# Windowed attention and SwiGLU on one core: the RMS weight row first, half-block scores for the first two query blocks, and a new plan

## The chip, the cores and the metric

The kernel runs on one core of a Trainium2 chip. A core has five engines with a queue each: TensorE (matmuls, PE in the profile; its weight loads are shown as PEld), VectorE (DVE), ScalarE (ACT), GpSimd (POOL) and SyncE (SP), which here only issues DMAs. Sixteen DMA engines move data between HBM and the core's SBUF. Matmuls write to PSUM, which has eight banks of 512 f32 values per partition. The metric is the device time in microseconds (us); lower is better.

## The reference

Inputs are q, k and v of shape (4, 8, 768, 64) in f32: four batches, eight heads, 768 positions, 64 values per head. Attention is causal with a window of 128 positions and four sink positions that every query sees:

```python
scores = scale * np.matmul(q, k.transpose(0, 1, 3, 2))
keep = is_sink | in_window            # pos < 4, or 0 <= query - key < 128
a = softmax(np.where(keep, scores, -1e9))
attn = np.matmul(a, v)
x = attn.transpose(0, 2, 1, 3).reshape(3072, 512)
xn = x / sqrt(mean(x * x) + 1e-6) * rms_g
out = (silu(xn @ w_gate) * (xn @ w_val)) @ w_out   # d_ff = 1536
```

The result is 3072 x 512 in f32. What attention gives is not stored; it stays on the core as the x of the second part.

## The kernel before

**Tiling.** The 3072 tokens are 24 blocks of 128, numbered g = 0 to 23, six to a batch (t = g mod 6). A block of keys is seen by its own block of queries (mask: upper triangle) and by the next one (mask: lower triangle). So for each key block, scores are computed transposed, keys on the partitions, for two query blocks at once: n = 0 is the own block, n = 1 the next. One block has eight heads; `u` is a half of them (four), `hi` the upper or lower 64 partitions of the transposed q and k. Four token blocks form a group G of the feed-forward part (six groups). Its hidden size of 1536 is 12 chunks `ft` of 128.

**Stages of a block.** q and k are loaded, transposed (on TensorE for blocks 0 to 7, `pe_t` with `copy_t`; by DMA from SP after that), scored (`scores`), exponentiated on ScalarE (`exps`), masked, multiplied with V (`av`, with the sink positions as an extra matmul from t = 2 on), divided by the sum of the weights (`normal`), squared for the mean (`square`), scaled by the inverse RMS and the weight row (`rms`, which gives `xr`), and transposed to `xnt` (`pe_x` or `dma_x`). The feed-forward part is then gate matmuls `g` (weights `wg`), value matmuls `v` (`wv`, `mms` at L863), tanh on ScalarE (`th`, L870), two VectorE products (`p`, L876, and `hT`, L886), and the output projection `o` (L896). In the profile the V of attention and the value matmul's PSUM are both called v; the line tells them apart.

**Masks.** There are three ways to mask. For g below `PE_MASKS` a matmul (`mask_bias`, L450) puts -32768 into the PSUM banks before the scores are added. For blocks up to `POOL_MASK_FROM`, and for the first of each batch, VectorE multiplies the exps by 0/1 masks (`mask_dve`, L533, one instruction per half of the heads, both n). From `POOL_MASK_FROM` on, GpSimd selects (`mask_pool`, L538 for n = 0, L543 for n = 1, two instructions per half of the heads).

**The weight row.** `rms_g` is 512 values in one row (`grow`). A matmul of a column of ones with the row spreads it over 128 partitions (`unit_gb`, L411), and `scale_gb` scales it into `gb`, which `rms` reads (L613).

**Loads.** k and q of block 0 are loaded in f32 by SP (L327) and cast on an engine (L331). All other q, k, v (L335, L339) and weight loads (`wg` and `wv` L381, `wo` L387) cast to bf16 on the way and are issued by GpSimd in the order of the string `LOADS`: `q-1` is q of block 1, `qkv-2` the three of block 2, `w-0-2` chunks 0 and 1 of `wg`, then of `wv`. `DEPTH` 8 makes the n-th of these loads wait for the landing of the (n-8)-th.

**What sets the order.** Nothing is issued as it is written. Each operation is entered in `Plan` with its engine or engines, an assumed duration, what it needs and gives, a priority, and the PSUM banks that it takes and drops. `Plan.run` is a list scheduler: at each step it takes, over all engines, the operation whose assumed start is earliest, then the one of lowest priority number. The order found is then the order of each engine's instructions, and it picks the PSUM bank of each tile. On the chip each engine takes its own instructions in that order and waits on semaphores; the assumed durations play no part there. `gate_of` holds scores of block 8 and later back until a feed-forward chunk (`GATE_LEAD` chunks ahead) has been planned.

`SPLIT` names blocks 0 and 1: their scores are two operations, one per n, in the same four PSUM banks, whose columns are laid out by half of the heads and pair of n (two heads x 256). So an exp of one n reads half a bank (128 x 256), eight of them per block.

`WARM` is 30: matmuls on zeros that fill idle time of TensorE at the start.

Of the kernel before, what the change touches and what calls it, by code (L numbers as in the profile page):

```python
# [26 lines left out]
class Plan:  # L27
# [2 lines left out]

    LATE = 300
    RESERVE = 8
    HOP = {"PE": 40, "ACT": 35, "DVE": 35, "POOL": 90, "SP": 60}
    START = {"PE": 800, "ACT": 800, "DVE": 1030, "POOL": 1290, "SP": 800}

# [5 lines left out]
    def op(self, ways, needs=(), gives=(), prio=0.0, takes=(), drops=(), ring=None, work=0.0,  # L43
           mode=0):
        self.ops.append(dict(
            ways=ways, needs=set(needs), gives=tuple(gives), prio=prio, takes=tuple(takes),
            drops=tuple(drops), ring=ring, work=work, mode=mode, at=len(self.ops), ready=0,
        ))

    def land(self, ring, first, work):  # L50
# [19 lines left out]
    def run(self):  # L70
        free, users = dict(self.START), {}
        self.loads = sum(o["ring"] == "POOL" for o in self.ops)
        wait = {o["at"]: set(o["needs"]) for o in self.ops}
        cand = {e: [] for e in free}
        left = len(self.ops)
        for o in self.ops:
            for t in o["needs"]:
                users.setdefault(t, []).append(o)
            if not o["needs"]:
                for e in o["ways"]:  # L80
                    cand[e].append(o)
        busy, warm, mode, order = [], False, 0, []
        while left:
            first = None

            many = min(
                (o for o in cand["PE"] if len(o["takes"]) > self.RESERVE), default=None,
                key=lambda o: o["prio"],
            )
            for e, found in cand.items():  # L90
                for o in found:
                    k = len(o["takes"])
                    if k > len(self.banks):
                        continue
                    ready = o["ready"] + self.HOP[e] if o["ready"] else 0
                    if k:
                        ready = max(ready, sorted(self.banks.values())[k - 1] + 40)
                    start = max(free[e], ready)
                    if (k and many and o["prio"] > many["prio"] and start > many["ready"]
                            and len(self.banks) - k < len(many["takes"])):  # L100
                        continue
                    key = (start, o["prio"], ready, o["at"])
                    if first is None or key < first[0]:
                        first = key, e, o
            if first is None:
                raise RuntimeError("stuck: %s" % [
                    (o["gives"], list(wait[o["at"]])) for o in self.ops if o["at"] in wait
                ][:20])
            (start, *_), e, o = first
            for x in o["ways"]:  # L110
                cand[x].remove(o)
            wait.pop(o["at"])
            left -= 1
            ns, lat, fn = o["ways"][e]
            if e == "PE":
                busy = [(a, d) for a, d in busy if a > start - 3413]
                warm = start - free[e] < 4000 and (warm or sum(d for a, d in busy) > 3000)
                ns = ns if warm else 2 * ns
                if o["mode"] != mode:
                    ns, mode = ns + 110, o["mode"]  # L120
                busy.append((start, ns if mode != 2 else 0))
                lat = ns + 180
            for s in o["takes"]:
                i = min(self.banks, key=lambda i: (self.banks[i], i))
                del self.banks[i]
                self.held[s] = i
            free[e] = start + ns
            end = start + lat
            if o["ring"] is not None:
                end = self.land(o["ring"], end, o["work"]) + self.LATE  # L130
            for s in o["drops"]:
                self.banks[self.held[s]] = end + 12
            for t in o["gives"]:
                for x in users.pop(t, ()):
                    x["ready"] = max(x["ready"], end + 12)
                    w = wait[x["at"]]
                    w.discard(t)
                    if not w:
                        for way in x["ways"]:
                            cand[way].append(x)  # L140
            order.append((start, end, e, fn, o))
        return order
# [3 lines left out]
def kernel(  # L146
# [31 lines left out]
    SW = P // HP  # L178
    inv_sqrt_d = 1.0 / math.sqrt(D)
    F32_LOADS = ("ks0","qs0")  # L180
    GROW = "SP"
    CAST_DVE = 600
    MASKS_PRIO = -5
    POOL_AT = (1,2)
    DEPTH = 8
    LOADS = "q-1 k-1 v-0 w-0-2 v-1 qkv-2 qkv-3 w-2-4 w-4-6 w-6-8 w-8-9 w-9-10 w-10-12 qkv-4 wo-0-6 qkv-5 wo-6-12 qkv-6 qkv-8 qkv-7"
    LOADS += "".join(f" qkv-{g}" for g in range(9, NB))
    PE_MASKS = 2
    POOL_MASK_FROM = 16
    X_DMA_FROM = 8  # L190
    QK_DMA_FROM = 8
    LD = 16
# [1 line left out]
    LOAD_LEAD = 10  # L194
    LEAD_FROM = 10
    WARM = 30
    GATE_LEAD = 14
    T_LEAD = 4
    SPLIT = (0,1)
    CHUNKS = (4,2,2)  # L200
    GB_PRIO = 2000
    FUSE_FROM = 2
    GROW_PRIO = -80
    MERGE = (2,)

    const = ctx.enter_context(tc.tile_pool(name="const", bufs=1))
# [49 lines left out]
    def either(ways, *args, **kw):  # L256
        op({e: (ns, ns + LAT[e], fn) for e, (ns, fn) in ways.items()}, *args, **kw)
# [68 lines left out]
        T["st", name, g] = opool.tile([P, H, D], FP32, name="stage", tag="osb")  # L326
        eng.dma_start(out=T["st", name, g], in_=block_of(src, g))  # L327

    def cast(name, g, copy):
        T[name, g] = ld.tile([P, H, D], BF16, name=name)  # L330
        copy(out=T[name, g], in_=T.pop(("st", name, g)))  # L331

    def load_bf16(name, src, g):
        T[name, g] = ld.tile([P, H, D], BF16, name=name)
# [10 lines left out]
    for i, name in enumerate(F32_LOADS):  # L345
        n, g, e = name[0], int(name[2:]), {"s": "SP", "a": "ACT"}[name[1]]
        src, eng = q if n == "q" else k, {"SP": nc.sync, "ACT": nc.scalar}[e]
        op({e: (430, 1000, lambda n=n, src=src, g=g, eng=eng: load_f32(n, src, g, eng))},
           (), [(n + "st", g)], -90 + i, ring="HW", work=970)
        either({"DVE": (CAST_DVE, lambda n=n, g=g: cast(n, g, nc.vector.tensor_copy)),  # L350
                "ACT": (640, lambda n=n, g=g: cast(n, g, nc.scalar.copy))},
               [(n + "st", g), "table"], [(n, g)], -99)
    op({GROW: (430, 1000, lambda: {"SP": nc.sync, "ACT": nc.scalar}[GROW].dma_start(
        out=grow, in_=moe_rms_g.rearrange("(o d) -> o d", o=1)))}, (), ["grow"], GROW_PRIO,
        ring="HW", work=50)
    act(1290, None, (), ["table"], -80)

    issue = []
# [81 lines left out]
    def dma_t(n, g):  # L440
        b, t = divmod(g, NT)
        nc.sync.dma_start_transpose(
            out=qk_tile(b)[:, "qk".index(n), :, t * P:(t + 1) * P],
            in_=T.pop((n, g)).rearrange("p h d -> p (h d)"),
        )

    def mask_bias(g):
# [100 lines left out]
    def av(g, u):  # L548
        b, t = divmod(g, NT)
        pv = bank(("av", g, u))  # L550
        if t >= 2:
            nc.tensor.matmul(  # L552
                out=pv[:, 0:HW], lhsT=T["esk", g], rhs=T["vsk", b][:, 4 * u:4 * u + 4, :],
                start=True, stop=False, skip_group_check=True,
            )
        for j in range(2):
            for hi in range(2):
                h = 4 * u + 2 * j + hi
                x = 2 * hi + j
                dest = pv[:, (h - 4 * u) * VW:(h - 4 * u + 1) * VW]  # L560
                if t >= 1:
                    nc.tensor.matmul(  # L562
                        out=dest, lhsT=T["e", g - 1, u][:, x, 1, :],
                        rhs=V16[b][:, t - 1, h, :],
                        start=(t == 1), stop=False, skip_group_check=True,
                    )
                own = (T["e", g, u][:, x, 0, :] if t + 1 < NT
                       else T["el", g][:, hi * HP + 2 * u + j, :])
                nc.tensor.matmul(  # L569
                    out=dest, lhsT=own, rhs=V16[b][:, t, h, :],  # L570
                    start=(t == 0), stop=True, skip_group_check=True,
                )
        T.pop(("e", g - 1, u), None)
# [130 lines left out]
    def block_scores(g):  # L704
# [2 lines left out]
        nq = 2 if t + 1 < NT else 1  # L707
        pa = -1000.0 + 10 * g
        early = -20.0 + g if g < 2 * GB else 0.1 * g
        slots = [("s", g, u, hi) for u in range(2) for hi in range(2)]  # L710
        parts = [(0, 1), (1, 2)] if g in SPLIT else [(0, nq)]
        if g < PE_MASKS:
            pe(864, lambda g=g: mask_bias(g), [("bias", 0), ("bias", 1), "ident", "idnos"]
               + ([("qp", g), ("kp", g)] if g else []), [("mb", g)], pa, takes=slots)
# [47 lines left out]
    for g in range(NB):  # L762
# [8 lines left out]
            old += [("ss", b - 2, i) for i in ((2, 4) if b - 2 < 2 else (2,))]  # L771
        for n in "qk":
            if g < QK_DMA_FROM:
                pe(225, lambda n=n, g=g: pe_t(n, g), [(n, g), "ident"] + old, [(n + "p", g)],
                   pa, takes=[(n, g)])
                ways = {"DVE": (345, lambda n=n, g=g: copy_t(n, g, nc.vector.tensor_copy)),
                        "ACT": (470, lambda n=n, g=g: copy_t(n, g, nc.scalar.copy))}
# [247 lines left out]
```

## Time and profile before

| | |
|---|---|
| median of 11 runs | 245.17 us (244.77 to 245.89) |
| the profiled execution's own time | 245.15 us |
| its span (first to last instruction) | 243.4 us |
| TensorE busy | 235.1 us (97% of the span), 2116 matmuls |
| VectorE busy | 180.9 us (74%) |
| ScalarE busy | 131.2 us (54%) |
| GpSimd busy | 89.6 us (37%) |
| chain that ended last | TensorE 92%, VectorE 4%, ScalarE 1% |
| gate, value and output matmuls | 69.5, 71.1 and 65.4 us busy |
| VectorE masks (L533) | 26, 0.68 us each |
| GpSimd selects (L538) | 10, 0.64 us each |
| casting loads (L335, L339) | 70, issue 0.88 us each, 11.7 to 12.7 us from issue to landing |

A line of the profile gives the start (in a timeline) and the duration, the engine, the source line, the operation, `out<-in` by the program's names, shapes, and in brackets how long the engine was idle before it and what ended that. In the row of slices each digit is the busy share of a 6.1 us slice, in tenths. [...] A matmul's duration overlaps the next one's, so the spacing of starts tells more than the duration.

### The profile page before, as it was taken

What the parts mean: (1) busy time and instruction counts of PE and PEld (TensorE: products, weight loads), DVE (VectorE), ACT (ScalarE), POOL (GpSimd) and SP (SyncE); (2) the same over time, 40 slices, a digit from 0 to 9 for tenths busy, and PEclk for the clock granted to TensorE, in tenths of its full rate; (3) what the DMA queues carried; (4) which work ended last, traced back from release to release, by engine and by line L of the source; (5) the groups of instructions that cost most, each with busy time, mean ns of one, the idle gap of its engine ahead of it and who ended that gap; (6) DMA issues with size and microseconds to landing.
All of it is one profiled execution on the core that took longest, in us unless ns stands there. A gap on an engine that the chain in (4) does not pass through costs nothing.

```text
span 243.4 us, 5513 instructions
## 1 busy us (share of the span) xinstructions
PE 235.1 (97%) x2116; PEld 148.4 (61%) x2116; DVE 180.9 (74%) x481; ACT 131.2 (54%) x268; POOL 89.6 (37%) x116
## 2 busy tenths in 40 slices
PE   4988999999999999999999999999999999999994
PEld 2557997885788875587796544544554444444443
DVE  4269979996999999998898889896379760377700
ACT  4677565869684827575734574573553311333111
POOL 8986875596445556245511130321320000000000
PEclk9999999999999999999999999999999999999999
DMA  9999999999999999999999561110231002200022
GB/s 130 150 168 196 186 187 187 159 138 177 147 196 151 158 133 155 161 227 143 133 152 117 111 172 24 22 22 30 81 108 24 1 0 86 86 3 0 0 86 86
DMA packets 113579, 27.35 MB, mean 112 GB/s; under 512 B 103697, under 2 KB 110609, under 8 KB 113554
## 3 DMA queue, kind: packets, MB, share of 16 engines
q0 software_dynamic: 81760, 13.90, 78.6%
q1 hardware_dynamic: 31650, 12.99, 29.3%
q8 instruction: 16, 0.26, 0.4%
q10 hardware_dynamic: 144, 0.13, 0.2%
q14 instruction: 9, 0.07, 0.1%
HBM read 28.31 MB, written 6.29 MB: 142 GB/s over the span
## 4 chain that ended last, share of the span: by engine, by line
PE 92%; DVE 4%; ACT 1%; issue 1%; POOL 1%; POOLq 0%; DVEq 0%
PE v L863 25%; PE o L896 25%; PE g L863 25%; PE s L468 4%; PE av L569 2%; PE av L562 2%; PE s L450 1%; PE av L552 1%; PE o_last L914 1%; ACT e L516 1%; PE k L428 1%; PE gb L411 1%; PE q L428 1%; PE x L628 1%; DVE xr L613 1%
## 5 line engine op out<-in xcount | busy, mean ns | idle before, releaser
L863 PE MATMUL v<-xnt,wv 128*128 128x128 bf16 (+2 forms) x528 | 71.1, 282 | 0.0
L870 ACT ACTIVATE th<-g 128x512 bf16<-128x512 f32 x72 | 43.2, 599 | 49.2 <-PE g L863 46.6
L863 PE MATMUL g<-xnt,wg 128*128 128x128 bf16 (+2 forms) x528 | 69.5, 282 | 0.0
L896 PE MATMUL o<-wo,hT 128*128 128x512 bf16 x276 | 65.4, 379 | 0.0
L876 DVE SCALAR_TENSOR_TENSOR p<-th,g 128x512 bf16<-128x512 bf16 x72 | 48.0, 682 | 21.2 <-ACT th L870 20.9
L863 PEld LDWEIGHTS <-wg 128*128 128x128 bf16 x528 | 43.1, 98 | 19.1 <-issue 0.4
L863 PEld LDWEIGHTS <-wv 128*128 128x128 bf16 x528 | 43.0, 98 | 19.2 <-issue 0.5
L886 DVE TENSOR_TENSOR hT<-p,v 128x512 bf16<-128x512 bf16 x72 | 47.2, 680 | 1.5 <-PE v L863 0.7
L516 ACT ACTIVATE e<-s 128x512 bf16<-128x512 f32 (+1 forms) x88 | 43.8, 569 | 7.5 <-PE s L468 6.2
L896 PEld LDWEIGHTS <-hT 128*128 128x128 bf16 x276 | 25.3, 98 | 26.6 <-issue 1.5
L904 ACT ACTIVATE osb<-o 128x512 f32<-128x512 f32 x23 | 13.8, 601 | 23.6 <-PE o L896 23.6
L335 POOL DMA_DIRECT2D q<-in_q_dram x23 | 20.5, 891 | 14.5 <-DMA k<-in_k_dram 6.3
L339 POOL DMA_DIRECT2D v<-in_v_dram x24 | 21.3, 888 | 11.8 <-DMA q<-in_q_dram 10.3
L335 POOL DMA_DIRECT2D k<-in_k_dram x23 | 20.4, 886 | 14.1 <-DMA v<-in_v_dram 8.5
L581 DVE TENSOR_TENSOR x<-av,rden 128x256 bf16<-128x256 f32 x48 | 20.4, 424 | 1.6
L589 ACT ACTIVATE sq<-x 128x512 bf16<-128x512 bf16 x24 | 15.1, 630 | 11.2 <-DVE x L581 11.1
L613 DVE SCALAR_TENSOR_TENSOR xr<-x,r,gb 128x512 bf16<-128x512 bf16 x24 | 18.0, 751 | 0.9
L533 DVE TENSOR_TENSOR e<-e,masks 128x1024 bf16<-128x1024 bf16 x26 | 17.0, 684 | 1.4 <-ACT e L516 1.4
L538 POOL TENSOR_SCALAR_AFFINE_SELECT e<-e 128x512 bf16<-128x512 bf16 x10 | 6.4, 637 | 31.4 <-ACT e L516 15.9
L569 PE MATMUL av<-v,e 128*128 128x65 bf16 x192 | 16.9, 193 | 0.4 <-ACT e L516 0.3
L569 PEld LDWEIGHTS <-e 128*128 128x128 bf16 x192 | 13.0, 98 | 3.5 <-ACT e L516 0.7
L562 PE MATMUL av<-v,e 128*128 128x65 bf16 x160 | 15.0, 193 | 0.0
(75 smaller groups left out, 181.6 us busy)
## 6 DMA issues: line engine op xcount, KB each, us to landing
out_dram<-osb SPq DMA_DIRECT2D x23, 256.0 KB, 2.3
v<-in_v_dram POOLq DMA_DIRECT2D x24, 128.0 KB, 11.7
q<-in_q_dram POOLq DMA_DIRECT2D x23, 128.0 KB, 12.7
k<-in_k_dram POOLq DMA_DIRECT2D x23, 128.0 KB, 12.1
wo<-in_moe_w_out_dram POOLq DMA_DIRECT2D x2, 768.0 KB, 11.6
wg<-in_moe_w_gate_dram POOLq DMA_DIRECT2D x5, 256.0 KB, 7.8
wv<-in_moe_w_val_dram POOLq DMA_DIRECT2D x5, 256.0 KB, 8.0
stage<-in_k_dram SPq DMA_DIRECT2D x1, 256.0 KB, 3.4
```

What stands on the lines that cost most here:

```text
L335: nc.gpsimd.dma_start(out=T[name, g], in_=block_of(src, g))
L339: nc.gpsimd.dma_start(out=V16[b][:, t, :, 0:D], in_=block_of(v, g))
L516: nc.scalar.activation(out=T["e", g, u][:, 2 * hi:2 * hi + 2, n0:n1, :].rearrange("p x n c -> p x (n c)"), in_=ps.rearrange("p (j c) -> p ...
L562: nc.tensor.matmul(out=dest, lhsT=T["e", g - 1, u][:, x, 1, :], rhs=V16[b][:, t - 1, h, :], start=(t == 1), stop=False, skip_group_check=True,
L569: nc.tensor.matmul(out=dest, lhsT=own, rhs=V16[b][:, t, h, :], start=(t == 0), stop=True, skip_group_check=True,)
L581: nc.vector.tensor_tensor(out=T["x16", g][:, 4 * u:4 * u + 4, :], in0=pvv[:, :, 0:D], in1=rden.unsqueeze(2).to_broadcast((P, 4, D)), op=AL ...
L613: nc.vector.scalar_tensor_tensor(out=T["xr", g], in0=T.pop(("x16", g)).rearrange("p h d -> p (h d)"), scalar=r[:, 3:4], in1=gb, op0=ALU.mu ...
L863: nc.tensor.matmul(out=ps[:, i * n:(i + 1) * n], lhsT=w_sb[:, kt, ft * P:(ft + 1) * P], rhs=T["xnt", G][:, kt, cols], start=(kt == 0), sto ...
L870: nc.scalar.activation(out=T["th", key], in_=BANK[("g", key)], func=ACT.Tanh, scale=0.5,)
L876: nc.vector.scalar_tensor_tensor(out=T["p1", key], in0=T.pop(("th", key)), scalar=1.0, in1=BANK.pop(("g", key)), op0=ALU.add, op1=ALU.mult,)
L886: nc.vector.tensor_tensor(out=T[hk][:, i:i + n, cols], in0=T.pop(("p1", key)).rearrange("p (n c) -> p n c", n=n), in1=BANK.pop(("v", key)) ...
L896: nc.tensor.matmul(out=BANK[("o", G, tb)], lhsT=T["h", G, ft // 4][:, ft % 4, tb * P:(tb + 1) * P], rhs=wo[:, ft, :], start=(ft == 0), sto ...
```

## The change

The change has these parts.

- `grow` is loaded from ScalarE's queue with priority -99 (before: SP, third in its queue, -80), which puts it ahead of the activation table's load. `GB_PRIO` goes from 2000 to -100000, so its matmul and scale come as early as the row allows.
- Blocks 0 and 1 keep scores per query block in two banks of their own: `bias_part`, `scores_part`, `exps_part` and `mask_part` take n as an index, a bank holds four heads x 128 of one n, an exp reads a whole bank (128 x 512), and each n has its own biases. `av` reads the new tiles `ep`.
- The cast of q of block 0 is two halves (`HALVES`), on either VectorE or ScalarE.
- `LOADS`: chunks 0 and 1 of `wg` and `wv` go ahead of v of block 0, and block 2's q, k and v ahead of v of block 1.
- `PE_MASKS` 2 to 3: block 2 is masked by bias matmuls, not by VectorE.
- `POOL_MASK_FROM` 16 to 14: blocks 14 and 15 are masked by GpSimd, not by VectorE.
- `GATE_LEAD` 14 to 15. `HOLD` adds to or takes from an operation's start in the scheduler's choice alone, for five operations. `CAST_DVE`, `MASKS_PRIO` and `POOL_AT` change assumed costs and priorities.
- The whole plan is made anew with these.

```diff
     LATE = 300
     RESERVE = 8
+    HOLD = {
+        ('th', (0, 0, 0)): -100,
+        ('qT', 3): 900,
+        ('wg', 6): -600,
+        ('s', 2, 0): -600,
+        ('mb', 0, 1): -900,
+    }
...
+            hold=self.HOLD.get(gives[0], 0) if gives else 0,
...
-                    key = (start, o["prio"], ready, o["at"])
+                    key = (start + o["hold"], o["prio"], ready, o["at"])
...
-    GROW = "SP"
-    CAST_DVE = 600
-    MASKS_PRIO = -5
-    POOL_AT = (1,2)
+    CAST_DVE = 1500
+    MASKS_PRIO = -20
+    POOL_AT = (0,2)
     DEPTH = 8
-    LOADS = "q-1 k-1 v-0 w-0-2 v-1 qkv-2 qkv-3 w-2-4 w-4-6 w-6-8 w-8-9 w-9-10 w-10-12 qkv-4 wo-0-6 qkv-5 wo-6-12 qkv-6 qkv-8 qkv-7"
+    LOADS = "q-1 k-1 w-0-2 v-0 qkv-2 v-1 qkv-3 w-2-4 w-4-6 w-6-8 w-8-9 w-9-10 w-10-12 qkv-4 wo-0-6 qkv-5 wo-6-12 qkv-6 qkv-8 qkv-7"
...
-    PE_MASKS = 2
-    POOL_MASK_FROM = 16
+    PE_MASKS = 3
+    POOL_MASK_FROM = 14
...
-    GATE_LEAD = 14
+    GATE_LEAD = 15
...
-    GB_PRIO = 2000
+    GB_PRIO = -100000.0
+    HALVES = ("qs0",)
+    HALF = set()
...
-    op({GROW: (430, 1000, lambda: {"SP": nc.sync, "ACT": nc.scalar}[GROW].dma_start(
-        out=grow, in_=moe_rms_g.rearrange("(o d) -> o d", o=1)))}, (), ["grow"], GROW_PRIO,
-        ring="HW", work=50)
+    op({"ACT": (430, 2100, lambda: nc.scalar.dma_start(
+        out=grow, in_=moe_rms_g.rearrange("(o d) -> o d", o=1)))}, (), ["grow"], -99)
...
+    def bias_part(g, n):
+        for hi in range(2):
+            nc.tensor.matmul(
+                out=bank(("s", g, n, hi)), lhsT=ident if g % NT else idnos,
+                rhs=bias[:, n:n + 1, :].to_broadcast((P, HP, P)),
+                start=True, stop=False, skip_group_check=True,
+            )
+
+    def scores_part(g, n):
+        b, t = divmod(g, NT)
+        qkT = T["qkT", b]
+        for hp in range(HP):
+            for hi in range(2):
+                pr = slice(hi * D, (hi + 1) * D)
+                nc.tensor.matmul(
+                    out=(BANK.get(("s", g, n, hi)) or bank(("s", g, n, hi)))[:, hp * P:(hp + 1) * P],
+                    lhsT=qkT[pr, 1, hp, t * P:(t + 1) * P],
+                    rhs=qkT[pr, 0, hp, (t + n) * P:(t + n + 1) * P],
+                    start=g >= PE_MASKS, stop=True, skip_group_check=True,
+                )
...
+    def exps_part(g, n, hi):
+        if ("ep", g, n) not in T:
+            T["ep", g, n] = epool.tile([P, H, P], BF16, name=f"e{n}", bufs=3)
+        nc.scalar.activation(
+            out=T["ep", g, n][:, hi * HP:(hi + 1) * HP, :].rearrange("p x c -> p (x c)"),
+            in_=BANK.pop(("s", g, n, hi)), func=ACT.Exp, scale=inv_sqrt_d,
+        )
...
+        if g in SPLIT:
+            for n in range(2):
+                slots = [("s", g, n, hi) for hi in range(2)]
+                biased = g < PE_MASKS
+                if biased:
+                    pe(432, lambda g=g, n=n: bias_part(g, n),
+                       [("bias", n), "ident", "idnos"] + ([("qp", g + n), ("kp", g)] if g else []),
+                       [("mb", g, n)], pa + 10 * n, takes=slots)
...
+            return
```

## The prediction

> **What bounds the kernel now.** I read the page first: busy shares, slices, chain.
>
> ```profile
> span 243.4 us, 5513 instructions
> PE 235.1 (97%) x2116; PEld 148.4 (61%) x2116; DVE 180.9 (74%) x481; ACT 131.2 (54%) x268; POOL 89.6 (37%) x116
> ...
> PE   4988999999999999999999999999999999999994
> ...
> POOL 8986875596445556245511130321320000000000
> ...
> DMA  9999999999999999999999561110231002200022
> ```
>
> TensorE is full from the fourth slice to the last but one. Its largest releaser rows in the chain of waits (2.1 us for the bias matmul, 1.1 for the first warm-up, 0.8 for transposed x) all lie before 28 us. So a microsecond saved on another engine after that is worth nothing, and a new wait of TensorE is paid in full: no hole stands behind it in which the queue could catch up.
>
> TensorE's timeline shows the last hole of the front:
>
> ```profile
> 26.82 0.94 PE L863 MATMUL v<-xnt,wv 128*128 128x128 bf16 x14
> 27.89 0.40 PE L628 MATMUL x<-ident,xr 128*128 128x128 bf16 x4
> 28.12 1.06 PE L863 MATMUL v<-xnt,wv 128*128 128x128 bf16 x16
> ```
>
> The v chunk ends about 27.6 and the transpose waits for xr until 27.89. In front of this, loads set the pace. Adding to each issue its own time to landing: v of block 0 is there at 9.4, wg 0-2 at 10.6, wv 0-2 at 11.9, v1, q2, k2, v2 at 13.0, 13.9, 14.8, 15.8, q3 and k3 at 16.6 and 17.4, wg and wv 2-4 at 19.2 and 20.6, wv 6-8 at 25.9, wv 10-12 at 31.5. TensorE first uses the last at 32.6.
>
> Then GpSimd's timeline where its load issues end, and VectorE's and TensorE's there. Columns: start, duration, engine, line, operation, tiles, count, wait before it:
>
> ```profile
> 113.42 0.88 POOL L339 DMA_DIRECT2D v<-in_v_dram  x1
> 115.01 0.88 POOL L335 DMA_DIRECT2D q<-in_q_dram  x1 [0.72 <-DMA k<-in_k_dram]
> 116.73 0.88 POOL L335 DMA_DIRECT2D k<-in_k_dram  x1 [0.84 <-DMA v<-in_v_dram]
> 117.59 0.88 POOL L339 DMA_DIRECT2D v<-in_v_dram  x1
> 118.86 0.63 POOL L538 TENSOR_SCALAR_AFFINE_SELECT e<-e 128x512 bf16<-128x512 bf16 x1 [0.38 <-ACT e L516]
> 119.45 0.63 POOL L543 TENSOR_SCALAR_AFFINE_SELECT e<-e 128x512 bf16<-128x512 bf16 x1
> ```
> ```profile
> 115.64 1.29 DVE L533 TENSOR_TENSOR e<-e,masks 128x1024 bf16<-128x1024 bf16 x2 [0.44 <-ACT e L516]
> ```
> ```profile
> 114.31 1.03 PE L896 MATMUL o<-wo,hT 128*128 128x512 bf16 x4
> 115.27 0.61 PE L468 MATMUL s<-qkT 64*128 64x256 bf16 x8
> 115.81 1.04 PE L896 MATMUL o<-wo,hT 128*128 128x512 bf16 x4
> 116.69 0.27 PE L552 MATMUL av<-vsk,esk 128*128 128x260 bf16 x1
> ```
>
> The two VectorE multiplies are block 14's masks. They end at 116.9; its attention-times-V (av, from 116.69; its first half needs the first multiply only) doesn't wait. GpSimd issues its last load (block 23's v) from 117.59 to 118.47 and only then has its first masks, block 16's. The loads wait for the landing of the eighth load before them, so they sit late by design.
>
> **What the Trainium skill says.** "PSUM — Partial Sum Buffer", Engine vs sequencer instructions: ScalarE's, VectorE's and GpSimd's queues are strict FIFO, and matmuls start in program order. The trace agrees: block 16's masks start only after the 117.59 issue. "DMA: Bandwidth & Descriptors", SWDGE vs HWDGE: a DMA that casts is GpSimd's alone, and all issuers share 16 engines; here every q, k, v and weight load that casts is a POOL row. Same page, Anatomy of one DMA: a fixed cost near 2 us; this trace has 3.4 for the first 256 KB. "TensorE: Matmul & The Clock Gate", What's actually happening: cold half-clock until some 3.4 us of activity; here four 128x512 matmuls take 1.87 us at 4.16 and later 0.86.
>
> **Part 1, the front.** The weight row's DMA goes from SP (1.95) to ScalarE, ahead of the table load. Its issue is about 0.5 us (0.46 and 0.57 for SP's two f32 loads; 0.61 for this row), so the 1.28 us table load ends near 2.6 instead of 2.1; the first cast waits for its data until 4.21, which hides it. SP's queue behind it is empty until 48, so leaving SP saves nothing. The matmul (2.07, cold) now stands at the head of TensorE, before every bias matmul and transpose. It starts when the row lands: the trace shows no landing, the page's 2 us after an issue at 0.8-1.3 gives 3.0 as an estimate (taken); the late end is 5.5, where SP's second f32 load has landed. From 3.0: matmul to 5.1, four bias matmuls (1.87) to 6.9, four transposes of 0.43 to 8.7, half scores 0.5 to 9.2. The q0 cast in two halves saves about 0.3, hidden by those bias matmuls.
>
> That looks 1.5 us better than before's first av at 13.06, but v0 now lies behind wg and wv 0-2. The bytes are the same, so it lands in the slot of 11.9; q2, k2, v2, v1 take 13.0, 13.9, 14.8, 15.8. Then: av of block 0 at 12.0; x done 1.5 later (as 13.06 to 14.57), 13.5. The rms ops stand on VectorE behind the copy of k2 and sink k (13.9 + 0.4 transposes + 0.45 copy + 0.6), so 15.4; xr 1.83 later (as 15.64 to 17.47), 17.2: a gain of 0.25. Block 1's x (four ops, 1.2) 18.4; its square 0.8 on ScalarE, behind which block 2's exps now stand: from 19.2 (before 19.53). Six ScalarE ops (2.7, as 19.53 to 22.20) and a 0.6 copy give block 1's xnt at about 22.5; the second g chunk starts at 22.6, before at 23.14.
>
> This gain is spent at once. Block 2's x transposes are moved ahead of v chunk 4. Its x is done about 24.1-24.3, xr 2.65 later (as 25.20 to 27.84), 26.7-26.95, while TensorE gets there at 26.2-26.5. After it 0.23 + 2 x 0.89: both v chunks end at 28.75-28.95, before at 29.01. Part 1 is worth -0.1 (-0.25 to 0; a landing near 4 instead of 3 would make it +0.3).
>
> Block 2's mask by TensorE (PE_MASKS 3) adds four bias matmuls (0.9-1.9 us) at about 14.7, under the wait for v1 (15.8); if that cover went they'd cost their length. It takes 1.29 us of VectorE multiplies at 21.41 away; xr of block 1, not these, holds the transposes there, so nothing more. The other score and exp edits keep 16 128-wide matmuls per block and make 16 exps of 256 into 8 of 512 (about 8 x 0.29 against 4 x 0.53 a block), inside the same wait for v. HOLD, GATE_LEAD and the plan's costs and priorities act only through the orders named here; elsewhere TensorE's queue is full and the same matmuls in another order cost the same.
>
> **Part 2, the masks of blocks 14 and 15.** POOL_MASK_FROM 14 takes four multiplies of 0.68 from VectorE (no gain: TensorE waits for none of them) and adds eight selects, 0.59 apart, to GpSimd. In the built program GpSimd has, after block 22's v load: three of block 15's selects, block 23's q load, the fourth select, block 23's k and v loads, and only then block 14's four. (Block 15's scores come before block 14's in both plans.) From the trace's end of the 113.42 issue, 114.30: selects 1.77 to 116.1; q (its gate opens by 115.0) 0.88 to 117.0; select 0.59; k (gate 116.7) 0.88 to 118.4; v 0.88 to 119.3; block 14's first select 0.63 to 120.0. Even without gates these are serial.
>
> TensorE's new order is o, o, scores 16, av 14, the same three pieces as the lines above have from 114.31, so av 14 comes at 116.7 as before; the sink and neighbour matmuls ahead of the first own one take 0.1. Its weight load of block 14's e waits for GpSimd, with everything behind it. Stall: 120.0 + 0.05 (a handover) - 116.8 = 3.2 us.
>
> What is late next: av 14's second half follows 0.3 + 0.87 later, at 121.2, when its first select (121.2) is just done; block 15's second half needs the fourth (121.8) and comes at 121.85. Block 16's exps wait for av 14 (120.4 and 121.6), its selects then run to 124.2, its av at 123.1 and 124.3 find them. VectorE's xr of blocks 14 and 15 slip by 5 us, to 126.0 and 131.5; their transposing DMAs land some 6 later, by 138, and are used at 140.7 + 3.2. Nothing more. Block 23's loads slip by up to 1.8 us; SP's transposes read them only from 142 on. Bounds: each microsecond that block 22's v issue moves moves the stall by one; its waits come from landings 15 to 18 us after issue, so I give it 1.2 either way: 2.0 to 4.4.
>
> **Sum.** Profiled execution: 245.15 (span 243.4 and 1.75 around it), practically the median of 245.17. 245.15 - 0.1 + 3.2 = 248.25; against the median 248.3.
>
> **Rivals.**
> - The weight row lands at 5.5. Then matmul to 7.5 and transposes to 11.1; av 0 at 14.3 instead of 12.0, partly absorbed by the ScalarE chain: xr 18.5 instead of 17.2, block 2's xr 28.0; part 1 is +1.0, the sum 249.3. For it: the row's own landing is unseen. Against: it leads its own queue.
> - The loads run earlier at 100-116, and the stall is 1 to 2: 246.6. For: gates depend on other traffic's landings. Against: no transfer before there is removed.
> - Not slower: block 22's v load is issued by 110.2, 3.2 us sooner, so that block 14's selects are done when TensorE comes at 116.8. Then the price is part 1 alone, between -0.6 (all holes of the front closed; the landing of wv 10-12 at 31.5 against its use at 32.6 caps it near 1) and +0.6: about 245.0. Against: GpSimd then was held by landings (1.97 us before 111.47), and five instructions stay ahead.
>
> **How the numbers follow.** Forecast case 0.62 (its own range 247.3 to 249.1), late row 0.12, half stall 0.14, no stall 0.12. The range 246.0 to 249.7 leaves out the last case and the far end of the second. Under 0.2% (0.5 us) this kernel's measurement can't tell a change: the no-stall case splits into 0.06 faster, 0.05 same, 0.01 slower; all others are slower: 0.89.
>
> **What would show it.** A wait of TensorE's av on GpSimd's e select of about 3 us near 117, the largest in the chain of waits after 28 us; block 14's select starting after the last load issue, 119-120; VectorE emptier at 107 and 115; v chunks 4 ending at 28.7-29.0; the weight row's matmul near 3.0. The forecast falls if that select starts before 117, or if the front moves by more than 1 us.

## The result and the profile after

The changed kernel takes 249.81 us, median of 12 runs (247.44 to 251.04), against 245.25 us (244.55 to 246.49, 47 runs) for the kernel before: 1.0176 times as long, 95% interval 1.0156 to 1.0195. Its profiled execution took 250.07 us with a span of 248.4. Every ratio here and below compares fast runs, which leaves out runs more than 1.5% above the fastest of the same kernel (two of experiment 2, one each of 7 and 12), so the medians of 2 and 7 lie above their ratios.

The page of the kernel after, its busy shares and slices:

```profile
span 248.4 us, 5522 instructions
PE 237.3 (96%) x2120; PEld 149.0 (60%) x2120; DVE 177.7 (72%) x477; ACT 130.2 (52%) x259; POOL 93.9 (38%) x124
...
PE   7889999999999999997699999999999999999994
...
POOL 8985865686246454439900203330310000000000
PEclk9999999999999999999799999999999999999999
```

TensorE's row has a hole that was not there: 7 and 6 in the nineteenth and twentieth slices, 112 to 124 us, beside a GpSimd that is at 9 there. Right in it the granted clock shows a 7. (GpSimd's share counts the 0.9 us that each issue of a load takes.) From the fourth slice on everything else is as before: full to the last slice but one.

TensorE's waits after 29 us hold one entry; the kernel before had none there:

```profile
PE av L624 <- POOL e L591: 3.5, 1, 3.5
```

GpSimd's timeline of the kernel after (start, duration, engine, line, operation, tiles):

```profile
113.53 0.88 POOL L350 DMA_DIRECT2D v<-in_v_dram  x1
114.41 0.65 POOL L591 TENSOR_SCALAR_AFFINE_SELECT e<-e 128x512 bf16<-128x512 bf16 x1
...
116.17 0.89 POOL L346 DMA_DIRECT2D q<-in_q_dram  x1
117.07 0.65 POOL L596 TENSOR_SCALAR_AFFINE_SELECT e<-e 128x512 bf16<-128x512 bf16 x1
117.66 0.89 POOL L346 DMA_DIRECT2D k<-in_k_dram  x1
118.54 0.88 POOL L350 DMA_DIRECT2D v<-in_v_dram  x1
119.42 0.66 POOL L591 TENSOR_SCALAR_AFFINE_SELECT e<-e 128x512 bf16<-128x512 bf16 x1
```

The first four selects are block 15's, then come block 23's loads between and behind them, and the select at 119.42 is block 14's first. GpSimd is never idle here; it is simply a queue with seven other instructions between block 22's v and the select that is wanted. TensorE's timeline in the same place:

```profile
116.42 0.19 PE L616 MATMUL av<-v,e 128*128 128x65 bf16 x1
120.14 0.20 PE L624 MATMUL av<-v,e 128*128 128x65 bf16 x1 [3.53 <-POOL e L591]
...
122.36 0.41 PE L605 MATMUL av<-vsk,esk 128*128 128x260 bf16 x1
...
123.02 1.90 PE L944 MATMUL g<-xnt,wg 128*128 128x256 bf16 x8
```

The first own matmul of block 14 (L624) would follow its neighbour's (L616) by 0.03; it comes 3.69 late. And then there is something that the waits don't list: eight gate matmuls take 1.90 where the same eight took 1.04 in the kernel before:

```profile
118.96 1.04 PE L863 MATMUL g<-xnt,wg 128*128 128x256 bf16 x8
```

The table of stretches shows why. A row gives the stretch, its length, the busy time of PE, PEld, DVE, ACT and POOL, then the granted clock, the DMA share and GB/s:

```profile
116.50:120.10 3.60, 0.11 (x2) 0.00 (x0) 0.00 (x0) 0.00 (x0) 3.59 (x6) 1.00 1.91 141
120.10:121.40 1.30, 1.26 (x15) 0.78 (x16) 0.61 (x2) 0.87 (x2) 1.30 (x3) 1.00 2.76 80
121.40:124.80 3.40, 3.40 (x36) 2.77 (x35) 1.82 (x6) 1.91 (x5) 2.81 (x5) 0.50 1.78 156
124.80:130.00 5.20, 5.20 (x61) 4.68 (x60) 4.47 (x13) 2.40 (x5) 0.00 (x0) 1.00 1.45 120
```

TensorE idles at full clock, works 1.3 us at full clock, and then has half its clock for 3.4 us, while it is 100% busy. That costs half of 3.4, 1.7.

The front, in TensorE's timeline, before and after:

```profile
24.92 1.95 PE L863 MATMUL g<-xnt,wg 128*128 128x128 bf16 x32
29.01 3.74 PE L863 MATMUL g<-xnt,wg 128*128 128x128 bf16 x64
```
```profile
24.32 2.18 PE L944 MATMUL g<-xnt,wg 128*128 128x128 bf16 x32
26.50 0.40 PE L683 MATMUL x<-ident,xr 128*128 128x128 bf16 x4
26.73 1.95 PE L944 MATMUL v<-xnt,wv 128*128 128x128 bf16 x32
28.52 3.74 PE L944 MATMUL g<-xnt,wg 128*128 128x128 bf16 x64
```

TensorE is 0.60 ahead where the second g chunk starts, and 0.49 ahead where the two v chunks end (28.52, before 29.01): the hole before block 2's x is shorter, but the g chunk in front of it now has a short stop of its own. The next landmark that both kernels have, block 15's sink scores (L726, before L671), starts at 112.71 instead of 113.09.

So for the profiled executions: 245.15 - 0.38 (front) + 3.69 (wait) + 1.70 (clock) = 250.16, and 250.07 was measured.

### The profile page after: what moved, and what is told of

Its sections match the earlier page's. It is cut to its first block, busy times and chain, and to the rows that moved or that the text cites. A ratio compares the mean times of both kernels' runs of the same rounds, so it can differ in the third digit from the quotient of the medians.

```text
span 248.4 us, 5522 instructions
## 1 busy us (share of the span) xinstructions
PE 237.3 (96%) x2120; PEld 149.0 (60%) x2120; DVE 177.7 (72%) x477; ACT 130.2 (52%) x259; POOL 93.9 (38%) x124
## 4 chain that ended last, share of the span: by engine, by line
PE 50%; POOL 1%; DVE 0%; issue 0%
PE g L944 15%; PE o L977 15%; PE v L944 15%; PE av L624 1%; PE o_last L995 1%; PE s L521 1%; PE av L616 1%; PE av L605 1%; POOL v L350 0%; POOL k L346 0%; POOL e L591 0%; PE s L537 0%; DVE last L1006 0%; PE ss L726 0%; PE vs L708 0%
## 5 line engine op out<-in xcount | busy, mean ns | idle before, releaser
L944 PE MATMUL g<-xnt,wg 128*128 128x128 bf16 (+2 forms) x528 | 70.9, 284 | 0.5 <-DMA wg<-in_moe_w_gate_dram 0.5
L569 ACT ACTIVATE e<-s 128x512 bf16<-128x512 f32 x72 | 39.2, 607 | 10.7 <-PE s L521 5.4
L624 PE MATMUL av<-v,e 128*128 128x65 bf16 x192 | 17.1, 196 | 4.7 <-POOL e L591 3.5
L591 POOL TENSOR_SCALAR_AFFINE_SELECT e<-e 128x512 bf16<-128x512 bf16 x14 | 8.9, 639 | 26.6 <-issue 13.6
L635 DVE RECIPROCAL rden<-av 128x4 f32<-128x4 f32 x48 | 8.5, 176 | 14.4 <-PE av L624 14.4
L624 PEld LDWEIGHTS <-e 128*128 128x128 bf16 x192 | 13.3, 100 | 7.2 <-POOL e L591 3.7
L616 PE MATMUL av<-v,e 128*128 128x65 bf16 x160 | 15.3, 197 | 0.0
```

Of the source, the lines that this page charges most:

```text
L569: nc.scalar.activation(out=T["e", g, u][:, 2 * hi:2 * hi + 2, n0:n1, :].rearrange("p x n c -> p x (n c)"), in_=ps.rearrange("p (j c) -> p ...
L616: nc.tensor.matmul(out=dest, lhsT=(T["ep", g - 1, 1][:, y, :] if g - 1 in SPLIT else T["e", g - 1, u][:, x, 1, :]), rhs=V16[b][:, t - 1, h ...
L624: nc.tensor.matmul(out=dest, lhsT=own, rhs=V16[b][:, t, h, :], start=(t == 0), stop=True, skip_group_check=True,)
L944: nc.tensor.matmul(out=ps[:, i * n:(i + 1) * n], lhsT=w_sb[:, kt, ft * P:(ft + 1) * P], rhs=T["xnt", G][:, kt, cols], start=(kt == 0), sto ...
```

## The experiments

All are timed beside the kernel before on the same chip. The theory at the start: the loss is the place of block 14's selects in GpSimd's queue, plus what a cooled TensorE loses afterwards; the front is worth next to nothing. Its rivals: the new plan costs something elsewhere; masks on GpSimd are too slow wherever they stand; the clock falls for another reason.

**1. The front without the GpSimd masks.**

```diff
-    POOL_MASK_FROM = 14
+    POOL_MASK_FROM = 16
```

> The kernel after with POOL_MASK_FROM back at 16: block 14's and 15's masks are VectorE's again, the new front stays. Theory (the loss is the wait on GpSimd near 117 and what follows from it; the front gained 0.4): no wait of TensorE above 0.5 us between 29 us and the end, granted clock 1.0 throughout, span near 243.0, time 244.8. Rival (the new plan costs something of its own elsewhere): 245.4 or more with no wait near 117.

Measured: 245.15 us (14 runs), ratio 1.0004 (0.9987 to 1.0020); span 243.1 in the profile, no wait of TensorE above 0.2 after 29 us. The whole loss lies in part 2, and the new front can't be told from the old one in time. The 244.8 forecast here, 0.9984 times the kernel before beside it (245.19), lies just below the interval.

**2. The GpSimd masks without the front** (the kernel before, `POOL_MASK_FROM` 16 to 14).

> The kernel before with POOL_MASK_FROM 14 alone; its front and plan are the old ones. Theory: GpSimd again has three selects of block 15, then q, select, k, v of block 23's loads, then block 14's first select at 119 to 120.5; TensorE waits 3 to 4 us for it and runs at half clock for some 3 us after it; 250.2 us (248 to 251.5), the loss of the whole change plus the 0.4 that its front gained. Rival (the stall needs the new front's timing, which brings TensorE there earlier or the loads later): under 247.5.

Measured: 250.77 us, ratio 1.0159 (1.0106 to 1.0212), spans from 245.3 (clock 0.998) to 251.0 (0.977). The wait is 3.91 in the profile, block 14's first select starts at 119.73, and the half-clock stretch runs from 120.43 to 123.84, here from the restart on:

```profile
120.44 0.24 PE L569 MATMUL av<-v,e 128*128 128x65 bf16 x1 [3.91 <-POOL e L538]
```

Part 2 alone does what the change does. One thing more came out: with the old front this execution reached block 15's sink scores at 112.63, before the profiled new front. Two executions of one front differ by as much as the two fronts do.

**3. Block 14's selects ahead of two more loads.**

```diff
         ('mb', 0, 1): -900,
+        ('q', 23): 5000,
+        ('k', 23): 5000,
+        ('v', 23): 5000,
```

> The kernel after with both blocks' masks on GpSimd as in it, but block 23's q load stands behind all of block 15's selects, and its k and v loads behind block 16's. Theory (place in the queue is what counts, not the engine): block 14's first select starts near 117.0 instead of 119.4, TensorE waits 1.0 to 1.5 us, too short for the clock to fall: span 244.0 to 244.6, time 246.1. Rival (a select is too slow for this place whatever stands ahead of it): a wait of 3 us or more, 249 or more.

Measured: 246.42 us, ratio 1.0054 (1.0036 to 1.0072), clock 0.997 or more in all eight runs. TensorE's timeline:

```profile
117.75 0.20 PE L627 MATMUL av<-v,e 128*128 128x65 bf16 x1 [1.04 <-POOL e L594]
```

Block 14's first select starts at 117.05, where it was forecast, and the wait shrinks to 1.04 (some 0.6 of that because block 22's v was issued at 112.92 here). The engine isn't the matter; the place is.

**4. TensorE fed through the wait.** In `av`, ahead of the sink matmul:

```diff
+        if (g, u) == (14, 0):
+            for _ in range(60):
+                nc.tensor.matmul(
+                    out=pv[:, HW:HW + P], lhsT=zeros, rhs=zeros, start=True, stop=True,
+                    skip_group_check=True,
+                )
```

> The kernel after with 60 matmuls of zeros by zeros (128 columns, some 0.055 us each, 3.3 in all) put on TensorE just ahead of block 14's first attention-times-V, into columns of its bank that nobody reads. TensorE still waits for the same select, but is busy for most of that time. Theory (idling lets the clock fall to half afterwards, and that costs 1.7 us on average): block 14's first own matmul still near 120.1, granted clock 1.0 right after it, time near 248.2 and runs closer together than the kernel after's. Rival (the clock falls at that place for another reason, or the lost time has nothing to do with the clock): the dip to 0.5 stays, time 249.8 or more.

Measured: 248.18 us (247.64 to 249.11), ratio 1.0120 (1.0096 to 1.0143). The table of stretches of this kernel:

```profile
116.50:120.00 3.50, 3.50 (x68) 3.49 (x67) 0.00 (x0) 0.00 (x0) 3.49 (x6) 1.00 2.12 138
120.00:121.40 1.40, 1.35 (x21) 0.90 (x19) 0.64 (x3) 1.15 (x3) 1.40 (x4) 1.00 1.77 125
121.40:124.80 3.40, 3.40 (x57) 3.13 (x55) 2.94 (x14) 2.81 (x7) 2.33 (x4) 1.00 2.26 133
```

The useful work waits nearly as before (the own matmuls come at about 119.7), but the clock stays at 1.00 where it was 0.50. (One of the six runs, 249.11, has a mean clock of 0.990.) The medians of the kernel after and of this one differ by 1.63 us, as forecast. That is the clock's share to within some tenths, since the wait was about 0.3 shorter here; and it comes from idling, since 60 matmuls that compute nothing take it away.

**5. The weight row back on SP**, its matmul back behind the transposes (`GB_PRIO` 2000); masks on VectorE as in 1.

> The front with the masks back on VectorE (as in the first of these kernels), and the weight row's DMA back on SP and its matmul back behind the transposes; loads and all else as there. Theory (loads set the front's pace; the row's place hides under the wait for block 0's v, and the order of loads carries the front's 0.3 to 0.4): block 0's av still near 11.6 to 12.0, span within 0.2 of 243.1, time 245.1. Rival (the row's early matmul, which warms TensorE and frees ScalarE's multiply, is what gained): block 0's av or block 0's xr 0.5 or more later, span 243.4 or more.

Measured: 245.56 us (21 runs), ratio 1.0007 (0.9996 to 1.0018), span 243.6. In time nothing can be told. In the trace, one execution, the rival is right: block 0's av starts at 12.65 (11.84 in experiment 1), its x at 18.37 (17.45), and the chunks end at 29.15 (28.62). TensorE's timeline shows how:

```profile
6.49 2.07 PE L428 MATMUL gb<-grow,ones 1*128 1x512 f32 x2
8.49 0.82 PE L445 MATMUL q<-ident,q 128*128 128x128 bf16 x6
```

The row's 2 us matmul stands between k's and q's transposes, and pushes block 0's first scores back. So in these traces the row's early place moved the front by up to 0.9 us at 18; the wait for v of block 0 doesn't hide it fully.

**6. The old order of loads**, plan made anew (`LOADS` as in the kernel before); masks on VectorE.

> The front with the masks back on VectorE, and the old order of GpSimd's loads (v of block 0 ahead of the first weights, v of block 1 ahead of block 2's q, k, v); the plan is made anew from it, so TensorE's order in the first 29 us changes with it. Theory (the order of loads carries the front's gain): the two v chunks of 128 columns end 0.3 to 0.4 later, span 243.4, time 245.4. Rival (the gain comes from the half scores, the masks by TensorE or the transposes ahead of the chunk): span within 0.15 of 243.1.

Measured: 248.24 us, ratio 1.0124 (1.0105 to 1.0142). Neither forecast: 3 us slower than experiment 1. The profile shows why this can't be put down to the loads: the new plan has another order on every engine, and TensorE gets four waits between 29 and 112 that no other kernel here has (0.7 for k of a later block, 0.5 and 0.4 for ScalarE's exps, 0.4 for wg). It doesn't isolate anything; experiment 11 does.

**7. One load less ahead** of block 14's selects (block 23's v alone gets a hold of 4000).

> The kernel after with block 23's v load alone put behind block 16's masks: one 0.88 us issue less ahead of block 14's first select. Theory (the wait shrinks by that issue; the clock falls only where the idle stretch is long enough to fill some fixed interval, which 3.7 us nearly always does): wait 2.8, clock falls in some of the runs only, fastest run near 246.9, median 247.8. Rival (any wait of some us costs its half again in clock): wait 2.8 and every run with a granted clock under 0.995, median 249.0.

Measured: 248.94 us (247.54 to 251.27), ratio 1.0130 (1.0107 to 1.0154). TensorE's timeline and the table of stretches:

```profile
118.61 0.20 PE L625 MATMUL av<-v,e 128*128 128x65 bf16 x1 [1.85 <-POOL e L592]
```
```profile
116.00:119.40 3.40, 1.55 (x20) 0.84 (x19) 0.33 (x2) 0.40 (x1) 3.39 (x6) 1.00 2.17 131
119.40:122.80 3.40, 3.40 (x35) 2.56 (x33) 2.09 (x7) 2.38 (x6) 2.91 (x6) 0.50 1.75 129
122.80:126.20 3.40, 3.40 (x44) 3.10 (x43) 2.20 (x11) 1.45 (x4) 1.21 (x2) 1.00 1.90 163
```

The wait is shorter than forecast, 1.85, since block 22's v was issued at 112.87 here, 0.66 sooner than in the kernel after. Yet the clock falls in the profiled run, and for the same 3.4 us. Four of the five runs have a mean clock of 0.984 to 0.993, one has 1.0. (A mean doesn't say where the clock fell: of 99 runs of the kernel before beside these experiments, 11 have 0.991 to 0.993, at spans of 242.8 to 245.2.) My theory that only an idle stretch nearly as long as a fixed interval does it is wrong. The rival's price of half the wait is wrong too, though its median of 249.0 came about: 1.85 costs as long a stretch as 3.53.

**8. The wait doubled** by six selects on an unused tile ahead of block 14's first.

> The kernel after with six more selects of 0.59 us on GpSimd, on a tile that nobody reads, just ahead of block 14's first select: the wait is doubled. Theory (idling costs its own length once, and the clock's loss after it is bounded, since TensorE warms again within a fixed time of working): wait 7.2, half clock from the restart on for 3 to 6 us, 253.0 to 254.8 us, runs closer together than the kernel after's. Rival (the clock's loss grows with the idle time): twice the 2 us of the kernel after, 255.4 or more.

Measured: 254.88 us (254.58 to 255.96), wait 7.2, clock 0.972 to 0.984.

```profile
115.30:118.70 3.40, 1.19 (x12) 0.42 (x10) 0.00 (x0) 0.30 (x1) 3.39 (x5) 1.00 2.10 141
118.80:129.00 10.20, 5.36 (x45) 3.66 (x46) 2.43 (x8) 2.78 (x6) 8.65 (x15) 0.50 1.59 124
129.00:132.00 3.00, 3.00 (x41) 2.74 (x40) 2.03 (x9) 1.29 (x4) 0.00 (x0) 1.00 0.00 0
```

Half clock for 10.2 us, three times 3.4, of which TensorE worked 5.36: a loss of 2.7. Experiment 1's span with it, 243.1 + 7.2 + 2.7, gives 253.0; 252.8 was measured. Half clock while TensorE idles costs nothing, so the wait has doubled and the clock's loss in the profiled run went from 1.7 to 2.7, as the theory had it; the median is 0.1 above its range.

**9. Block 15's and 14's selects first, by holds** (block 22's three loads +5000, block 23's three +9000).

> The kernel after with block 15's four selects ahead of block 22's q load (its exps are done at 107.1, while GpSimd stands idle before the load of 110.2), block 14's four right behind that q load, and block 22's k and v loads and all of block 23's behind block 16's masks. Nothing else changes on GpSimd: the same selects, the same loads. Theory (only the place in the queue costs): block 14's first select starts near 114.8, when its exps are done; no wait of TensorE for it above 0.3 us, clock 1.0, 245.1 us (244.6 to 245.6). Rival (masks on GpSimd cost in themselves, or the late loads are missed at 142): 246 or more.

Measured: 254.18 us, ratio 1.0359 (1.0330 to 1.0388). Near 117 the theory held: no wait, clock 1.0. But the holds, and the plan made anew with them, put block 23's k at 174.5, its k's transposing DMA at 182.4 and its v at 193.9 (in the kernel after, the last of these loads is issued at 118.54). So block 23's av comes at 207.46, where the kernel after has it at 183.68, and its xr is done at 212.30. SP waits for that and issues the last x's transposing DMA:

```profile
212.33 1.20 SPq L701 DMA_TRANSPOSE xnt<-xr  x1
```

TensorE waits for it:

```profile
PE g L950 <- DMA xnt<-xr: 5.7, 1, 5.7
```

This wait, at 209 to 215, again brings half clock, from 211.59, inside it, to 218.42: 6.83 us, twice 3.4. The rival was right on the time, and the cause was the lateness, not the masks, as experiment 12 shows. (The expectation of experiment 12 puts this lateness down to SP's order; the trace has SP waiting for xr.)

**10. Block 2's bias matmuls left out** (masks on VectorE as in 1).

> The front with the masks back on VectorE, and block 2's four bias matmuls left out, so that its scores stay unmasked (that part of the computation is missing). TensorE's order is otherwise the same. Theory (they stand under the wait for block 1's v, which lands at 15.5): the wait for that v grows by their 0.9 us, span 243.1, time 245.1. Rival (they cost their length): span 242.2, time 244.3.

Measured: 245.24 us (22 runs), ratio 1.0003 (0.9991 to 1.0015). TensorE's waits for v before 29 us, first with the bias matmuls (experiment 1), then without:

```profile
PE av L624 <- DMA v<-in_v_dram: 1.1, 2, 1.0
```
```profile
PE av L626 <- DMA v<-in_v_dram: 2.9, 2, 1.9
```

Take the work away and the wait takes its place. They are hidden.

**11. The old order of loads with every other engine's order kept.** After the plan is made, GpSimd's first twelve loads change places:

```diff
+    for i, j in zip(at, (0, 1, 4, 2, 3, 8, 5, 6, 7, 9, 10, 11)):
+        order[i] = order[i][:3] + (was[j],) + order[i][4:]
```

> The front with the masks back on VectorE, every engine's order as there, only GpSimd's first twelve loads issued in the old order. Theory (the front hangs on block 2's q and k, whose copies stand ahead of block 0's rms on VectorE, and on the first weights): block 2's k lands 1.2 later, block 0's x transposes start 0.9 to 1.3 later than 17.4, the first g chunk is 0.3 to 1.0 later, span 243.3 to 244.0, time 245.4 to 246.1. Rival (with this order of the other engines the old loads do as well): 245.1 or less.

Measured: 246.24 us (13 runs), ratio 1.0030 (1.0013 to 1.0047), span 243.3 in the profile. Block 0's x transposes start at 17.96 (17.45 in experiment 1), half of what was forecast, and the first g chunk no longer waits for weights. The span is at the low end of the forecast, the median above it: five runs, the profiled one among them, had clock 1.0 and 245.3 to 245.9, while eight had 0.990 to 0.993 and 246.1 to 246.9. The order of loads does matter to this plan, but in the profiled run by 0.2 us only; why the clock is lower in most of the others, no profile here shows. (A candidate is a wait of 1.78 for block 1's q, until 13.02, which experiment 1 doesn't have.)

**12. Only GpSimd's queue changed.** The kernel after, every other engine's order kept, and blocks 22's and 23's six loads put behind block 16's last select:

```diff
+    late = [x for x in order if x[2] == "POOL" and x[4]["gives"][0] in
+            [(n, g) for g in (NB - 2, NB - 1) for n in "qkv"]]
+    order = [x for x in order if not any(x is y for y in late)]
+    at = max(i for i, x in enumerate(order)
+             if x[2] == "POOL" and x[4]["gives"][0][:2] == ("e", 16))
+    order[at + 1:at + 1] = late
```

> The kernel after, with every other engine's order kept instruction for instruction; on GpSimd alone the six loads of blocks 22 and 23 are put right behind block 16's masks (the run before deferred block 23's k and v far more, to 174 and 194 us, and the transposing DMAs of the last x stood on SP behind them). Theory (only the place in GpSimd's queue costs): block 15's selects run from 110 or earlier, block 14's start when its exps allow, near 115; the six loads are issued from about 120.6 to 125.9 and land before SP wants them from 136 on; no wait of TensorE above 0.3 us near 117 or after, granted clock 1.0, 245.1 us (244.7 to 245.6). Rival (masks of two blocks on GpSimd cost in themselves, or the later loads are late again): 246 or more.

Measured: 245.11 us (14 runs; one of them took 248.64, which no profile explains), ratio 0.9993 (0.9975 to 1.0011). GpSimd's timeline of this kernel, and TensorE's only listed wait after 29 us, which ends at 113.86:

```profile
111.51 0.63 POOL L596 TENSOR_SCALAR_AFFINE_SELECT e<-e 128x512 bf16<-128x512 bf16 x1
115.21 0.64 POOL L591 TENSOR_SCALAR_AFFINE_SELECT e<-e 128x512 bf16<-128x512 bf16 x1 [3.07 <-ACT e L569]
...
121.16 0.89 POOL L346 DMA_DIRECT2D q<-in_q_dram  x1
```
```profile
PE v L944 <- DVE p L957: 0.8, 1, 0.8
```

GpSimd now waits three microseconds for ScalarE instead of being waited for. The loads are issued from 121.16 on, block 22's ten microseconds later than in the kernel after, land in 4 to 6 us instead of 10 to 12, all by 131.2, and SP transposes them in time. With the same selects and the same loads on the same engine, the ratio goes from 1.0176 to 0.9993. No kernel here is measurably faster than the one before.

## Where the prediction was right, and the step that failed

**What bounds the kernel** held: TensorE is full after 29 us, and a wait put into it was paid in full (3.69), with nothing caught up.

**Part 1, the front.** The weight row's matmul started at 2.46 after 0.58 of waiting, where an estimate of 3.0 was taken from a figure that its page gives for DMAs of GpSimd, while this one is ScalarE's; the rival of a late row is out. Block 0's av at 11.76 (forecast 12.0), its x at 17.37 (xr forecast 17.2), the second g chunk at 22.53 (22.6), block 2's x at 26.50 (26.7 to 26.95), the chunks' end at 28.52 (28.75 to 28.95): each step is there within 0.6, the gain 0.4 to 0.5 in this execution instead of 0.1. The expected hold-up, block 2's xr at 26.7 or later, came at 26.44, about when TensorE got there. Not foreseen: the second half of the first g chunk waits 0.48 for weights, and block 0's x waits 0.50 for a VectorE product of block 1's x, its own xr being done at 16.76. The size is not settled: experiment 1's interval, -0.3 to +0.5 us, holds the forecast of -0.1 and not the 0.4 to 0.5 of this one execution. That block 2's masks are hidden is shown (experiment 10). One remark was too quick: that leaving SP "saves nothing" passes over the matmul's early place, which in experiment 5's trace is worth 0.5 at 29 us.

**Part 2, the wait.** The order on GpSimd, the place, and the waiting instruction are as forecast. Block 14's first select ended at 120.08, forecast 120.0; TensorE was there at 116.45 instead of 116.8. So the wait came to 3.69 instead of 3.2, inside the stated 2.0 to 4.4: the term was mis-sized mostly by TensorE's arrival, not by GpSimd's queue. Experiments 2, 3 and 12 leave no other cause.

**"What is late next ... Nothing more"** is the step that failed. What came next was on TensorE itself: the cooled clock. The prediction quoted the half clock for the start of the kernel, and put it at nothing, without a word, after a wait of 3 us in the middle. It is worth 1.7 per stretch of 3.4 us. That it was not always one stretch is in the runs of the kernel after: two with clock 0.998 to 1.0 have spans of 245.7 and 245.9; six with 0.991 to 0.993 have 247.1 to 248.9; four with 0.984 to 0.986 have 248.6 to 249.3. A clock of 0.992 over 248 us is 2 us missing, about one stretch; 0.985 is 3.7, about two; only the profiled run shows where. The waits seem to differ too: experiment 1's span of 243.1 and a wait of 3.5 make 246.6, so the two runs at full clock waited some 0.8 less (an estimate; neither was profiled). The forecast of 248.3 is what the wait alone would give (experiment 4, with the clock kept up, has 248.18); the median is 1.5 above it and just outside the range, 0.1 above its upper end; the ratio times the 245.17 that the prediction started from gives 249.5, just inside. That it lies so near is luck: the upper part of the range stood for a longer wait, of which 0.5 came about, or a late row, and not for the clock.

**The rivals.** "Half stall" and "not slower" didn't come about; the second describes experiment 12, where the selects are done in time and the price is part 1 alone, 245.1.

## What to carry to other kernels

Before moving work to a less busy engine, write down its queue around the place and ask what stands ahead of the moved instruction: the share of busy time (37% here) says nothing of it. Where the queue holds transfers that aren't needed for a long while, moving those back was free here as long as what is computed from them wasn't late (experiment 12 against 9). And where TensorE is the bound, price a long wait with a stretch of half clock on top: here 1.7 us, after waits of 1.85 and more in the profiled runs, and not after 1.04. Matmuls that fill the wait saved it (experiment 4).

## What the hardware showed unexpectedly

- **The clock goes in whole stretches.** Half clock lasted 3.41 us in the kernel after and in experiments 2 and 7, 6.83 in 9 and 10.2 in 8. The Trainium skill, "TensorE: Matmul & The Clock Gate", What's actually happening, gives a free-running window of 3413 ns, and the traces agree: the full-clock stretches are whole numbers of it too (36 between 124.83 and 247.72 in the kernel after). The same place names an idle window of about 3.4 us as the condition for the cold state; here a wait of 1.85 us was enough in experiment 7's profile, and no run of experiment 3, with 1.04 in its profile, has a mean clock under 0.997. The measurement decides.
- **What counts is how full one window is.** Cut at these windows, all fourteen profiles agree: once the clock was full, a window with less than 1.4 us of TensorE work was always followed by half clock, one with more than 1.6 never, and in between both occur (many of these windows lie at the kernel's end). The wait of 1.85 in experiment 7 fell into one window, which was left with 1.55 of work (the first of its rows above). The wait of 3.53 in the kernel after lay across two, 114.60 to 118.01 with 2.0 of work and 118.01 to 121.42 with 1.3, and the clock fell after the second only. So it seems that the price of a wait depends on where it falls; no run moved a wait against the windows.
- **The half clock can come late.** In the kernel after TensorE had been working for 1.3 us at full clock when it fell, at the next window's edge; in experiment 2 it fell as the work restarted. A slow stretch whose start shows no wait can have its cause some microseconds earlier.
- **A select can hold VectorE up.** In experiment 12 VectorE's timeline has

```profile
110.62 0.95 DVE L664 SCALAR_TENSOR_TENSOR r<-y,m 128x1 f32<-128x1 f32 x1
111.61 0.55 DVE L664 SCALAR_TENSOR_TENSOR r<-r,y 128x1 f32<-128x1 f32 x1
```

where the kernel after has 0.22 and 0.16 for the same two. They run beside block 15's selects (109.75 to 112.14) and end with them; TensorE then waits 0.83 for a VectorE product, until 113.86. The Trainium skill, "SBUF — State Buffer", SBUF: two separate sides, says that a VectorE instruction with two SBUF inputs and a GpSimd instruction that reads SBUF shut each other out of a shared port. The trace agrees, and shows the other direction too: a select that starts at 134.52 in experiment 12, beside an xr of VectorE begun at 134.42, takes 1.15 instead of 0.63. It wasn't tested by itself.
